# Linear attention and SwiGLU on one core: batch 0 loaded in order and contracted by head pairs, batches 2 and 3 prepared later

## The chip, the core and the metric

The kernel runs on one core of a Trainium2 chip. The core has five engines, each with its own in-order instruction queue: PE (matrix multiply, with weight loads shown apart as PEld), DVE (vector), ACT (scalar functions), POOL, and SP, which here only issues transfers. Transfers run on 16 DMA engines. Those issued by SP stand in one queue and those issued by POOL in another; here POOL's bring the weights from float32 to bf16 on the way, and some of SP's transpose. The metric is the device time of one execution in microseconds; of several runs the median counts.

## The reference, cut to what matters

Eight batches of 8 heads, 576 positions and 64 values per head. The attention has no softmax: its sums over positions are taken first.

```python
def phi(x, c, s):                       # c, s: cos and sin of a position's angle
    r = np.maximum(x, 0.0)
    return np.concatenate([r * c, r * s], axis=-1)
q_p, k_p = phi(q, cos_w, sin_w), phi(k, cos_w, sin_w)
kv  = np.einsum('bhsf,bhsd->bhfd', k_p, v)
z   = np.sum(k_p, axis=2)
num = np.einsum('bhsf,bhfd->bhsd', q_p, kv)
den = np.einsum('bhsf,bhf->bhs', q_p, z)[..., None] + 1e-06
x   = num / den                         # then to 4608 rows of 512
xn  = x / sqrt(mean(x * x) + 1e-06) * rms_g
out = (silu(xn @ w_gate) * (xn @ w_val)) @ w_out      # 512 -> 1536 -> 512
```

## The kernel before

**Tiles and names.** Of a batch's 576 positions 512 make four tiles of 128 rows (j or c = 0 to 3). The last 64 are the rest; the rests of two batches share one tile (j = 4), so odd batches have five tiles and even ones four. raw holds a batch's q, k or v as it was loaded (8 heads on 128 partitions, six buffers), remq, remk and remv the rests. qp and kp are relu(q) and relu(k) times cos and sin in bf16, 128 columns per head; vv is v in bf16 with a column of ones, which makes z beside kv. There is one kp, one vv and one qpT (qp transposed) for all batches; qpr and qprT are the same for the rests of q.

**Attention of a batch.** k_prep and v_prep fill kp and vv. kvz multiplies them for four heads at a time (20 matmuls) into one PSUM tile and copies the result to kvzs. nd(b, j) multiplies qpT with kvzs into a PSUM tile of the pool att, which has one buffer. x_of(b, j) makes x from it: on DVE den, rec and the product xt; on ACT the sum of squares (scr, ssq); on POOL the power that gives rs. xn_scale multiplies xt with rs and gb on DVE; xn_tr transposes the result by a transfer on SP, xn_tr_pe on PE with a copy on ACT, into xnT.

**FFN.** Eight blocks, one per batch, and a ninth for the rests. A block has 12 steps. gval(blk, nn) is one: 8 matmuls (gps and vps, 128 x 512), silu on ACT (sil), a product on DVE (hT). gps and vps have two PSUM buffers each. outp(blk, ...) multiplies hT with w_out, 48 matmuls a block, 4 beside each gval of the next block; store copies the result (osb) and sends it out. Block 0's output projection stands by itself behind its gval, four PSUM tiles at once, with what batch 1 still lacks among its 12 steps.

**Order.** Nothing is reordered: each engine runs what the program lists for it, in that order, and the program is written out by hand. At the start the loads of q, k, v and the weights of gate and value (wg, wv) are issued, almost all by POOL; batch 0 is prepared and contracted, and block 0 starts tile by tile (first_steps). Then attention_beside(b, r) is called behind each step of the blocks: r counts steps from the start of block b - 1, and is negative in the blocks before it. Batch 2 (batch2_beside) and batch 3 are both prepared beside block 1, batch 4 to 7 each beside the last five steps of block b - 2 and the first nine of block b - 1.

**Queues.** POOL's queue holds the loads and the rs of every x_of, in the program's order: a load behind an rs waits until that x_of is done. SP's holds the transposes of q, rests and xn, and the stores. A queue's ninth transfer waits until its first has landed.

## Time and profile before

| | us |
|---|---|
| runs | 364.98, 369.48, 369.74 |
| median | 369.48 |
| the profiled execution | 370.0 |
| its span | 368.2 |
| granted PE clock, mean of the span | 0.962 |
| PE busy in the span | 322.9 (88%), 2096 matmuls |
| DVE, ACT, POOL busy | 197.2, 156.5, 98.0 |
| read from and written to HBM | 38.01 MB, 9.44 MB |

The span is what the trace covers, in one profiled execution; its own time, 370.0 us, is 1.8 us longer and half a microsecond above the median. Times in the timeline count from the span's start. A row gives start, duration, engine, line, operation, output <- inputs, shapes and a count; in brackets stands how long the engine was idle before it and which instruction or transfer ended that. Durations of two neighbours on an engine may overlap a little, so distances between starts say more than durations. A matmul is called gps, vps, acc, kvz, nd, tps (transpose of qp) or tpx (transpose of xn) by the tile that it writes.

### The profile page before, as it was taken

The page shows a single profiled execution, that of the slowest core. Times are in us where ns is not written, and L with a number is a line of the kernel's source. Part 1 is how long each engine was busy: PE and PEld are TensorE (multiplying, and loading weights), DVE is VectorE, ACT ScalarE, POOL GpSimd, SP SyncE. Part 2 cuts the span into 40 slices and gives each one's busy share as a digit, 9 for nine tenths or more (in the row PEclk, how much of TensorE's full clock was granted, in tenths as well). Part 3 has the DMA queues.
Part 4 walks back from the last instruction along what each step waited for, and adds up shares of the span by engine and source line. Part 5 has one row for each costly group of instructions (what it writes and reads, how often), then busy time and mean ns, then how long its engine had stood idle before and what let it go on. Part 6 is the DMA issues. An engine that isn't in the chain of part 4 may idle for free.

```text
span 368.2 us, 5681 instructions
## 1 busy us (share of the span) xinstructions
PE 322.9 (88%) x2096; PEld 161.3 (44%) x2096; DVE 197.2 (54%) x420; ACT 156.5 (43%) x310; POOL 98.0 (27%) x145
## 2 busy tenths in 40 slices
PE   0459998985854999999999999799899999999995
PEld 0448454432421544444445445344444444444442
DVE  3654576463694369747954795486567222323210
ACT  2725484585434344534363445242535232332321
POOL 8317320342244036404901490161011000000000
PEclk9856999998996999999999999999999999999999
DMA  7999999569279438995995899999513200001013
GB/s 229 242 208 211 256 306 268 120 181 199 40 145 174 113 94 163 217 212 127 189 257 158 172 204 108 201 170 204 116 45 73 71 28 30 28 28 59 30 57 86
DMA packets 61611, 53.58 MB, mean 146 GB/s; under 512 B 44944, under 2 KB 50064, under 8 KB 61584
## 3 DMA queue, kind: packets, MB, share of 16 engines
q0 software_dynamic: 13024, 32.51, 38.0%
q1 hardware_dynamic: 48560, 20.72, 28.9%
q8 instruction: 16, 0.26, 0.3%
q14 instruction: 11, 0.09, 0.1%
HBM read 38.01 MB, written 9.44 MB: 129 GB/s over the span
## 4 chain that ended last, share of the span: by engine, by line
PE 56%; DMA 16%; DVE 12%; ACT 8%; issue 4%; POOL 2%; ACTq 0%; SPq 0%; DVEq 0%; POOLq 0%
PE gps L310 17%; PE vps L310 17%; PE acc L347 15%; DMA raw<-in_v_dram 9%; DMA qpT<-qp 5%; PE kvz L199 3%; DVE hT L319 3%; ACT sil L318 2%; PE nd L227 2%; ACT scr L253 2%; ACT vv L137 2%; DVE kp L130 2%; POOL raw L91 1%; PE acc L546 1%; DVE rec L242 1%
## 5 line engine op out<-in xcount | busy, mean ns | idle before, releaser
L319 DVE TENSOR_TENSOR hT<-vps,sil 128x512 bf16<-128x512 f32 x108 | 74.3, 689 | 131.1 <-PE vps L310 90.6
L310 PE MATMUL gps<-xnT,wg 128*128 128x512 bf16 (+1 forms) x408 | 102.3, 376 | 7.2 <-ACT xnT L137 5.0
L310 PE MATMUL vps<-xnT,wv 128*128 128x512 bf16 (+1 forms) x408 | 102.4, 376 | 0.0
L347 PE MATMUL acc<-wo,hT 128*128 128x512 bf16 x384 | 96.7, 380 | 0.0
L318 ACT ACTIVATE sil<-gps 128x512 bf16<-128x512 f32 x108 | 63.8, 591 | 64.8 <-PE gps L310 64.8
L310 PEld LDWEIGHTS <-wv 128*128 128x128 bf16 x456 | 44.8, 101 | 51.5 <-issue 2.5
L258 POOL TENSOR_TENSOR rs<-ssq,mhalf 128x1 f32<-128x1 f32 x36 | 20.4, 566 | 167.3 <-ACT scr L253 167.3
L310 PEld LDWEIGHTS <-wg 128*128 128x128 bf16 x456 | 41.9, 100 | 48.2 <-issue 9.6
L347 PEld LDWEIGHTS <-hT 128*128 128x128 bf16 x384 | 37.7, 98 | 45.6 <-issue 0.5
L329 ACT COPY osb<-acc 128x512 f32<-128x512 f32 x36 | 20.8, 584 | 27.8 <-PE acc L347 26.1
L199 PE MATMUL kvz<-vv,kp 128*128 128x65 bf16 x320 | 15.1, 200 | 11.9 <-DVE vv L139 4.7
L137 ACT CAST vv<-raw 128x512 bf16<-128x512 f32 x28 | 16.2, 623 | 20.3 <-DMA raw<-in_v_dram 20.3
L227 PE MATMUL nd<-kvzs,qpT 128*128 128x65 bf16 x256 | 14.3, 200 | 8.7 <-DMA qpT<-qp 2.5
L199 PEld LDWEIGHTS <-kp 128*128 128x128 bf16 x320 | 13.4, 102 | 16.9 <-issue 5.8
L227 PEld LDWEIGHTS <-qpT 128*128 128x128 bf16 x256 | 12.3, 102 | 17.1 <-DMA qpT<-qp 3.0
L130 DVE TENSOR_SCALAR qp<-raw,cos_tab 128x512 bf16<-128x512 f32 x32 | 16.6, 528 | 3.2 <-issue 3.2
L91 POOL DMA_DIRECT2D raw<-in_q_dram x23 | 17.7, 775 | 1.1 <-POOLq L589 0.8
L91 POOL DMA_DIRECT2D raw<-in_v_dram x23 | 17.5, 761 | 1.9 <-DMA wo<-in_moe_w_out_dram 1.4
L91 POOL DMA_DIRECT2D raw<-in_k_dram x23 | 17.6, 764 | 0.2 <-issue 0.2
L130 DVE TENSOR_SCALAR kp<-raw,cos_tab 128x512 bf16<-128x512 f32 x32 | 15.6, 502 | 0.4 <-DMA raw<-in_k_dram 0.3
L170 PE MATMUL tps<-ident,qp 128*128 128x128 bf16 x64 | 6.2, 262 | 9.5 <-ACT qp L128 9.3
L310 PE MATMUL vps<-xnT_104,wv 128*128 128x512 bf16 x48 | 12.3, 379 | 0.0
(78 smaller groups left out, 250.7 us busy)
## 6 DMA issues: line engine op xcount, KB each, us to landing
out_dram<-osb SPq DMA_DIRECT2D x32, 256.0 KB, 3.0
raw<-in_q_dram POOLq DMA_DIRECT2D x20, 256.0 KB, 8.8
raw<-in_k_dram POOLq DMA_DIRECT2D x20, 256.0 KB, 4.1
raw<-in_v_dram POOLq DMA_DIRECT2D x20, 256.0 KB, 4.5
raw<-in_k_dram POOLq DMA_DIRECT2D x3, 1024.0 KB, 10.6
raw<-in_v_dram POOLq DMA_DIRECT2D x3, 1024.0 KB, 16.2
raw<-in_q_dram POOLq DMA_DIRECT2D x2, 1024.0 KB, 12.8
wg<-in_moe_w_gate_dram POOLq DMA_DIRECT2D x3, 512.0 KB, 16.9
```

The costliest lines, as they stand in the source:

```text
L91: eng.dma_start(out=raws[what, b][:, h0 : h0 + n, :], in_=src[b, h0 : h0 + n, 0:SM, :].rearrange("h (p j) d -> p h (j d)", j=NJ),)
L130: nc.vector.tensor_scalar(out=dst, in0=src, scalar1=tab[lanes, col : col + 1], scalar2=0.0, op0=ALU.mult, op1=ALU.max,)
L137: nc.scalar.copy(out=dst, in_=src)
L199: nc.tensor.matmul(ps[:, half, hh * DE : (hh + 1) * DE], lhsT=kp[:, c, h, :], rhs=vv[:, c, h, :], start=(c == 0), stop=(c == NJ),)
L227: nc.tensor.matmul(ps[rows, h // HH, (h % HH) * DE : (h % HH + 1) * DE], lhsT=src[:, h, cols], rhs=kz[:, h, :], start=True, stop=True,)
L253: nc.scalar.activation(out=scr[:, :], in_=xt[:, :], func=AF.Square, scale=DM**-0.5, accum_out=ssq[:, :],)
L258: nc.gpsimd.tensor_tensor(out=rs[:, :], in0=ssq[:, :], in1=mhalf[:, :], op=ALU.pow)
L310: nc.tensor.matmul(ps[:, c0 : c0 + n], lhsT=w[:, dt, nn * P : (nn + 1) * P], rhs=xnTs[blk][:, dt, c0 : c0 + n], start=(dt == 0), stop=(dt ...
L318: nc.scalar.activation(out=sil[:, :], in_=gps[:, :], func=AF.Silu)
L319: nc.vector.tensor_tensor(out=hTs[blk][:, nn, :], in0=vps[:, :], in1=sil[:, :], op=ALU.mult)
L329: nc.scalar.copy(out=osb[:, :], in_=acc[:, :])
L347: nc.tensor.matmul(acc[:, :], lhsT=hTs[blk][:, nn, j * P : (j + 1) * P], rhs=wo[:, nn, :], start=(nn == 0), stop=(nn == NNT - 1),)
```

## The change

**The start.** Batch 0's q comes in four pieces of two heads, k in two halves and v in four pieces, all from SP, in this order, with gb behind. POOL issues the rests of k and v, then copies one element of v's second piece (gate), and behind that copy the weights; the rest of q follows much later. v is cast by head pairs (v_prep_heads), and kvz_heads contracts two heads at a time (10 matmuls), ACT and DVE taking turns.

**Behind it.** Batch 1's v is loaded ahead of w_out. qr_prep of batches 0 and 1, k_prep and v_prep of batch 1 change steps, and kvz(1) moves from behind step 2 of block 0's output projection to behind step 0; nd, x_of, xn and their transposes each move one step ahead there. kvz(2, 0) moves a step later, and nd(1, 4), x_of and xn of the first pair of rests go from block 1 to the first two steps of block 2.

**Batch 3** gets a plan of its own: loads in halves in steps 3 to 8 of block 1 (before: quarters, from two steps before block 1 to its step 9), q from step 10 of block 1 (before: 7), k from step 11 (before: 8), v in steps 0 and 1 of block 2 (before: 10 of block 1 on), kvz in steps 2 and 3 (before: 1 and 2), nd from step 4 (before: 3).

**The plan.** The steps of batches 4 to 7 are the same as before, now from a table. Within a step the table's order is xn, q, k, v, kvz, nd; before it was q, k, v, kvz, nd, xn.

```diff
+    def v_prep_heads(b, h0, n, eng):
+        src = raws["v", b][:, h0 : h0 + n, :].rearrange("p h (j d) -> p j h d", j=NJ)
+        copy(eng, vv[:, 0:NJ, h0 : h0 + n, 0:D], src)
...
-    def kvz(b, half, eng=nc.scalar):
+    def kvz_heads(b, h0, n, eng):
...
+        g, hh = divmod(h0, HH)
+        for h in range(h0, h0 + n):
             for c in range(NJ + 1):
                 nc.tensor.matmul(
...
+    def kvz(b, half, eng=nc.scalar):
+        kvz_heads(b, half * HH, HH, eng)
...
-    load_piece("q", q, 0, 0, 2, nc.sync)
-    load_piece("q", q, 0, 2, 2, nc.sync)
-    load_piece("q", q, 0, HH, HH, nc.gpsimd)
-    nc.gpsimd.iota(iota_i[:, :], pattern=[[0, 1]], base=0, channel_multiplier=1)
-    masks.make_identity(nc, ident[:, :])
-    load("k", k, 0)
-    load("v", v, 0)
+    for e in range(4):
+        load_piece("q", q, 0, 2 * e, 2, nc.sync)
+    for e in range(2):
+        load_piece("k", k, 0, HH * e, HH, nc.sync)
+    for e in range(4):
+        load_piece("v", v, 0, 2 * e, 2, nc.sync)
...
+    nc.gpsimd.iota(iota_i[:, :], pattern=[[0, 1]], base=0, channel_multiplier=1)
+    masks.make_identity(nc, ident[:, :])
+    load_rest("k", k, 0, nc.gpsimd)
+    load_rest("v", v, 0, nc.gpsimd)
+    nc.gpsimd.tensor_copy(out=gate[:, :], in_=raws["v", 0][:, 2, 0:1])
     for s in range(0, DFF, 512):
         load_wgv(s)
-    load_rest("q", q, 0, nc.gpsimd)
...
-    for c in range(NJ + 1):
-        v_prep(0, c, A if c % 2 else V)
-    kvz(0, 0, A)
-    kvz(0, 1, V)
+    v_prep(0, NJ, V)
+    for e in range(4):
+        v_prep_heads(0, 2 * e, 2, A if e % 2 else V)
+        kvz_heads(0, 2 * e, 2, V if e % 2 else A)
...
-    load("q", q, 1)
-    load("k", k, 1)
-    load_wout(0)
-    load_wout(1)
-    load("v", v, 1)
-    load_wout(2)
+    load_rest("q", q, 0, nc.gpsimd)
+    for what, src in (("q", q), ("k", k), ("v", v)):
+        load(what, src, 1)
+    for s in range(3):
+        load_wout(s)
...
+    PLAN = plan_of(
+        xn=each(4, 5), q=each(-5, 5), k=each(-4, 5), v=((-2, (0, 1)), (-1, (2, 3)), (0, (4,))),
+        kvz=each(1, 2), nd=each(3, 5),
+    )
+    PLAN_3 = plan_of(
+        xn=each(5, 5), q=each(-2, 5), k=((-1, (0,)), (0, (1, 2)), (1, (3, 4))),
...
-        if r in (1, 2):
-            kvz(b, r - 1)
-        if 3 <= r <= 6:
-            nd(b, r - 3)
-            x_of(b, r - 3)
...
-        if 4 <= r <= 7:
-            xn(b, r - 4)
...
+        plan = PLAN_3 if b == 3 else PLAN
+        for what, n in plan.get(r, ()):
...
+        if b == 3 and r == 0:
+            nd(1, NJ)
+            x_of(1, NJ)
+        if b == 3 and r == 1:
+            xn(1, NJ)
...
-        if nn == 2:
+        if nn == 0:
             kvz(1, 0, A)
             kvz(1, 1, V)
```

Each row of the following lists is an instruction of one engine: line, operation, output <- inputs with their buffer numbers, shape.

ACT at the contraction of batch 0, before: the last two copies of qpT, k's sines, its share of v, and the copy of the first four heads of kvz.

```order
L137 COPY qpT_101<-tps_196 128x8x128
L137 COPY qpT_101<-tps_216 128x8x128
L128 ACTIVATE kp_94<-raw_123,sin_tab_107 128x8x64 x4
L137 CAST vv_95<-raw_127 128x8x64 x2
L137 CAST kvzs_242<-kvz_241 128x260
L253 ACTIVATE scr_299,ssq_300<-xt0_96 128x513
```

And now:

```order
L138 COPY qpT_101<-tps_201 128x8x128
L138 COPY qpT_101<-tps_221 128x8x128
L129 ACTIVATE kp_94<-raw_120,sin_tab_107 128x8x64 x4
L138 CAST kvzs_244<-kvz_243 128x130
L138 CAST vv_95<-raw_123 128x4x2x64
L138 CAST kvzs_244<-kvz_243 128x130
L138 CAST vv_95<-raw_123 128x4x2x64
L260 ACTIVATE scr_306,ssq_307<-xt0_96 128x513
```

The copy of a pair's kvz stands ahead of the cast of the next pair's v that this engine does.

DVE in block 1, from batch 2's second xn to its third, before: hT is the FFN's product, qp and kp with raw_899 and raw_1014 are batch 3's.

```order
L319 TENSOR_TENSOR hT_918<-vps_1189,sil_1198 128x512
L266 SCALAR_TENSOR_TENSOR xn_1208<-xt0_96,rs_1181,gb_93 128x512
L237 TENSOR_SCALAR den_1219<-nd_1210 128x8
L242 RECIPROCAL rec_1221<-den_1219 128x8
L245 TENSOR_TENSOR xt1_97<-nd_1210,rec_1221 128x512
L130 TENSOR_SCALAR qp_1230<-raw_899,cos_tab_106 128x8x64
L130 TENSOR_SCALAR qp_1230<-raw_899,sin_tab_107 128x8x64
L130 TENSOR_SCALAR kp_94<-raw_1014,cos_tab_106 128x8x64
L130 TENSOR_SCALAR kp_94<-raw_1014,sin_tab_107 128x8x64
L319 TENSOR_TENSOR hT_918<-vps_1237,sil_1246 128x512
L266 SCALAR_TENSOR_TENSOR xn_1255<-xt1_97,rs_1227,gb_93 128x512
```

And now:

```order
L326 TENSOR_TENSOR hT_924<-vps_1159,sil_1168 128x512
L273 SCALAR_TENSOR_TENSOR xn_1178<-xt4_100,rs_1154,gb_93 128x512
L244 TENSOR_SCALAR den_1189<-nd_1180 128x8
L249 RECIPROCAL rec_1191<-den_1189 128x8
L252 TENSOR_TENSOR xt0_96<-nd_1180,rec_1191 128x512
L326 TENSOR_TENSOR hT_924<-vps_1203,sil_1212 128x512
L273 SCALAR_TENSOR_TENSOR xn_1221<-xt0_96,rs_1197,gb_93 128x512
```

Batch 3's q and k are gone from these steps; hT, xn and x_of keep their order.

DVE in block 3, batch 4's second x_of (den, rec, xt) between two hT, before:

```order
L319 TENSOR_TENSOR hT_1781<-vps_1929,sil_1938 128x512
L237 TENSOR_SCALAR den_1954<-nd_1945 128x8
L242 RECIPROCAL rec_1956<-den_1954 128x8
L245 TENSOR_TENSOR xt4_100<-nd_1945,rec_1956 128x512
L266 SCALAR_TENSOR_TENSOR xn_1964<-xt3_99,rs_1925,gb_93 128x512
L319 TENSOR_TENSOR hT_1781<-vps_1970,sil_1979 128x512
```

And now:

```order
L326 TENSOR_TENSOR hT_1784<-vps_1932,sil_1941 128x512
L273 SCALAR_TENSOR_TENSOR xn_1948<-xt3_99,rs_1928,gb_93 128x512
L244 TENSOR_SCALAR den_1961<-nd_1952 128x8
L249 RECIPROCAL rec_1963<-den_1961 128x8
L252 TENSOR_TENSOR xt4_100<-nd_1952,rec_1963 128x512
L326 TENSOR_TENSOR hT_1784<-vps_1973,sil_1982 128x512
```

xn of the first tile moved from behind the second tile's x_of to ahead of it.

More of the change, by code (lines that the diff above doesn't have):

```diff
@@ L81 @@
     iota_f = consts.tile([P, 1], FP32, name="iota_f")
+    gate = consts.tile([P, 1], FP32, name="gate")
     mhalf = consts.tile([P, 1], FP32, name="mhalf")
@@ L445, with plan_of, each @@
     gval_end(0, 1)
-    load("q", q, 1)
-    load("k", k, 1)
-    load_wout(0)
-    load_wout(1)
-    load("v", v, 1)
-    load_wout(2)
+    load_rest("q", q, 0, nc.gpsimd)
[3 more added lines that the diff above has]
+        load_wout(s)
     for what, src in (("q", q), ("k", k), ("v", v)):
         load(what, src, 2)
+    def plan_of(**firsts):
+        plan = {}
+        for what, steps in firsts.items():
+            for r, ns in steps:
+                for n in ns:
+                    plan.setdefault(r, []).append((what, n))
+        return plan
+    def each(r0, n):
+        return [(r0 + i, (i,)) for i in range(n)]
+    PLAN = plan_of(
[4 more added lines that the diff above has]
+        xn=each(5, 5), q=each(-2, 5), k=((-1, (0,)), (0, (1, 2)), (1, (3, 4))),
+        v=((0, (0, 1, 2)), (1, (3, 4))), kvz=each(2, 2), nd=each(4, 5),
+    )
     def attention_beside(b, r):
@@ L460, in attention_beside @@
         pieces = {}
-        if b > 2:
+        if b == 3:
+            for i, (what, src) in enumerate((("q", q), ("k", k), ("v", v))):
+                for e in range(2):
+                    pieces[-9 + 2 * i + e] = (what, src, HH * e, HH)
+        if b > 3:
             for i, (what, src) in enumerate((("q", q), ("k", k), ("v", v))):
@@ L525 @@
         gval(0, nn)
-        if nn == 2:
+        if nn == 5:
             qr_prep(0)
+        if nn == 9:
+            qr_prep(1)
         if 6 <= nn <= 9:
@@ L535 @@
             k_prep(1, 1, V, A)
-            qr_prep(1)
+            k_prep(1, 2, V, A)
         if nn == 11:
-            for c in range(2, NJ + 1):
-                k_prep(1, c, V, A)
+            k_prep(1, 3, V, A)
+            k_prep(1, NJ, V, A)
+            for c in range(NJ + 1):
+                v_prep(1, c, A if c % 2 else V)
     for j in range(NJ):
         accs[0, j] = pools["gv"].tile([P, DM], FP32, name="acc", tag="gv"[j % 2])
-    for c in range(NJ + 1):
-        v_prep(1, c, A if c % 2 else V)
     for nn in range(NNT):
```

61 lines of the change are left out of this document (26 added, 35 removed).

## The prediction

> **What bounds the kernel now.** I read the windows by stage first (start:end, length, busy time and instructions of PE, PEld, DVE, ACT, POOL, then PE clock, DMA share, GB/s), then, for each window with an idle PE, the timeline of the engine that PE waited for. The first window is the start up to batch 0's first nd, the second the output projection of block 0, and each from 71.49 on one FFN block.
>
> ```profile
> 0.00:22.09 22.09, 6.69 (x73) 5.88 (x73) 10.40 (x38) 10.46 (x17) 10.45 (x19) 0.87 0.98 231
> ...
> 54.27:71.49 17.22, 14.98 (x139) 7.76 (x137) 10.70 (x25) 8.94 (x21) 3.63 (x6) 1.00 0.81 185
> 71.49:115.27 43.78, 28.48 (x201) 13.24 (x201) 26.23 (x57) 23.11 (x48) 16.72 (x24) 0.92 0.73 154
> 115.27:150.92 35.65, 35.65 (x233) 17.14 (x233) 23.68 (x51) 13.42 (x29) 13.35 (x19) 0.95 0.65 134
> 150.92:185.33 34.41, 33.59 (x217) 16.34 (x216) 23.40 (x50) 15.80 (x33) 14.16 (x21) 1.00 0.85 191
> 185.33:219.29 33.96, 33.96 (x233) 16.73 (x232) 24.04 (x51) 14.74 (x33) 13.36 (x19) 1.00 0.89 196
> 219.29:255.28 35.99, 33.49 (x218) 16.24 (x216) 23.32 (x50) 14.64 (x31) 9.59 (x15) 1.00 1.07 164
> 255.28:291.01 35.73, 34.29 (x234) 16.77 (x232) 19.48 (x39) 15.96 (x34) 2.75 (x5) 1.00 0.37 88
> ```
>
> PE is idle 15.4 us of the start and 15.3 us of block 1; from block 2 on it is the bound, with 0 to 2.5 us idle per block. Block 4 has no idle at all and takes 33.96 us, 2.83 a step: that is PE's own pace. So the change can win in the first 115 us, where it takes work out of block 1, and it can lose in blocks 2 to 6, where it puts that work and where PE has nothing left to give. Below I carry one number along, the lead: how much earlier than before PE stands at the same instruction (minus is earlier).
>
> **The start.** From the timeline (start, us, engine, line; in brackets the idle time before it and what ended it) and the DMA issues of the first 20 us (last number: us to landing):
>
> ```profile
> 1.28 0.92 POOL L91 DMA_DIRECT2D raw<-in_q_dram  x1 [0.83 <-POOLq L589]
> 8.54 2.56 ACT L128 ACTIVATE qp<-raw,sin_tab 128x512 bf16<-128x512 f32 x4 [4.49 <-DMA raw<-in_q_dram]
> 13.18 1.80 DVE L130 TENSOR_SCALAR kp<-raw,cos_tab 128x512 bf16<-128x512 f32 x4 [0.31 <-DMA raw<-in_k_dram]
> 14.13 2.56 ACT L128 ACTIVATE kp<-raw,sin_tab 128x512 bf16<-128x512 f32 x4
> 17.43 1.14 ACT L137 CAST vv<-raw 128x512 bf16<-128x512 f32 x2 [0.73 <-DMA raw<-in_v_dram]
> 19.82 0.38 ACT L137 CAST kvzs<-kvz 128x260 bf16<-128x260 f32 x1 [1.25 <-PE kvz L199]
> 20.24 1.26 PE L199 MATMUL kvz<-vv,kp 128*128 128x65 bf16 x20 [0.46 <-ACT kvzs L137]
> 28.89 0.59 PE L310 MATMUL gps<-xnT,wg 128*128 128x128 bf16 x4
> ```
> ```profile
> raw<-in_k_dram POOLq DMA_DIRECT2D x1, 1024.0 KB, 10.3
> raw<-in_q_dram SPq DMA_DIRECT2D x2, 256.0 KB, 2.8
> ```
> ```profile
> 2.00:4.00 2.00, 0.00 (x0) 0.00 (x0) 1.28 (x9) 0.59 (x4) 1.83 (x6) 1.00 1.01 297
> ```
>
> Today each stage waits for its load: q at 8.54, k at 13.18, v at 17.43. SP's two pieces of q land 2.8 us after issue, at 297 GB/s. Four 0.26 MB pieces at that rate take 0.88 us apart, so q is complete at 0.74 + 2.8 + 2.65 = 6.2; k's 1.05 MB and the two rests' 0.26 MB add 4.4 (10.6); v ends at 14.1. ACT then starts q 2.3 us earlier (8.54 - 6.2); its four qp, two copies and four kp follow one another as now, so it ends kp at 14.13 + 2.56 - 2.3 = 14.4, and DVE, free of q at 10.5, has its kp by then. From there v is no longer late; the chain of head pairs is the bound. Each pair is 10 matmuls (0.63 by the x20 row), a copy (about 0.3, from 0.38 for 260 columns) and the next pair's cast (0.42 to 0.6), which stands behind that copy on the same engine: PE, copy, cast, PE, one after the other. The waits that make it so are there today: the second half of kvz starts 0.04 us after ACT's copy of the first (19.82 + 0.38 to 20.24), though it writes another bank. Four times 0.63, four copies of 0.3, three casts of 0.5 and eight hand-overs of 0.07 make 5.8 us; nd starts at 20.2, not 22.09, where the first window ends: **-1.9** (ends: 0 if k comes 2 us later, -2.6 if the queue runs faster than 297).
>
> The weights wait behind the gate on POOL, with the rs operations behind them. The gate opens at about 11.6 (2.9 MB at 297 GB/s), the six issues end by 17, the first pair of weights (1 MB) lands by about 19, and is read at 28.89 - 1.9: nothing lost, and 8 us of cover if the gate opens late. Batch 0's rest of q goes onto POOL's queue behind batch 0's rs, ahead of batch 1's loads: one more issue in front of these, hidden, since batch 1's q is first read in step 6 of the block, four steps of gval on; its own reader, qr_prep(0), moved three steps later. w_out's issues move behind v1's two (0.75 us each, by the x3 row further down), and are first read at 54.27, ten steps on: hidden as well. The iota ahead of POOL's loads gives the tables 0.9 us earlier, which q hides. Two queues carry what one carried; gb, last on SP behind v, is read only by xn, which needs nd, x_of and rs first.
>
> The Trainium skill, DMA: Bandwidth & Descriptors, section Issuing engines are not separate DMA queues, says that issuing from other engines saves only issue time, since all run on the same 16 DMA engines. By that rule the start would win only the 0.92 us issue ahead of the iota, and the sum below would be 373.0. The 2.8 against 10.3 us rows speak for more.
>
> **The output projection of block 0.**
>
> ```profile
> 54.27 3.03 PE L546 MATMUL acc<-wo,hT 128*128 128x512 bf16 x12
> 57.51 0.42 DVE L139 CAST vv<-remv 64x512 bf16<-64x512 f32 x1
> 57.31 1.31 PE L199 MATMUL kvz<-vv,kp 128*128 128x65 bf16 x20
> ```
>
> kvz(1) moves from behind the third step to behind the first. But vv is done at 57.9 (57.51 + 0.42), whatever PE does: DVE and ACT carry the same q, k and v preparation as before from step 8 of the block on, qr_prep and k_prep only change places among the steps. So PE does 4 of these 12 matmuls (1 us), and then waits 2 us for vv where it waited almost nothing. The 8 matmuls it could have done there come behind kvz (8 x 0.25 = 2.0 by the x12 row, of which the wait before was nothing); the chain nd, x_of, xn starts behind two of these steps, and two bare steps stand behind it instead of one: **+2.0** (ends 0, if vv is ready sooner, and +2.5). The lead is then -1.9 + 2.0 = +0.1.
>
> **Block 1.**
>
> ```profile
> 74.54 0.60 ACT L318 ACTIVATE sil<-gps 128x512 bf16<-128x512 f32 x1
> 77.79 0.63 ACT L253 ACTIVATE scr<-xt_99 128x513 bf16<-128x513 f32 x1 [1.43 <-DVE xt_99 L245]
> 78.42 0.58 ACT L318 ACTIVATE sil<-gps 128x512 bf16<-128x512 f32 x1
> 87.44 0.64 PE L199 MATMUL kvz<-vv,kp 128*128 128x65 bf16 x16 [1.50 <-ACT vv L137]
> 91.94 1.03 PE L310 MATMUL gps<-xnT,wg 128*128 128x512 bf16 x4
> 115.27 1.87 PE L310 MATMUL gps<-xnT,wg 128*128 128x512 bf16 x4 [4.96 <-ACT xnT L137]
> ```
>
> ACT is the bound from 74.54 to 87.44. nd(1,4)'s square and the wait for it leave (1.43 + 0.63 + 0.1 = 2.2), so kvz(2) comes at 87.44 + 0.1 - 2.2 = 85.4. Step 5's gval now stands before it, hidden in that wait, and the next gval starts at 87.2, not 91.94: lead -4.7. Then the x_of steps:
>
> ```profile
> 98.69 0.69 DVE L245 TENSOR_TENSOR xt_96<-nd,rec 128x512 f32<-128x512 f32 x1
> 99.50 0.64 ACT L253 ACTIVATE scr<-xt_96 128x513 bf16<-128x513 f32 x1 [2.54 <-DVE xt_96 L245]
> 100.13 0.58 ACT L318 ACTIVATE sil<-gps 128x512 bf16<-128x512 f32 x1
> 100.74 0.69 DVE L319 TENSOR_TENSOR hT<-vps,sil 128x512 bf16<-128x512 f32 x1 [0.57 <-ACT sil L318]
> 101.35 0.74 DVE L266 SCALAR_TENSOR_TENSOR xn<-xt_96,rs,gb 128x512 bf16<-128x512 f32 x1
> 102.44 0.69 DVE L245 TENSOR_TENSOR xt_97<-nd,rec 128x512 f32<-128x512 f32 x1
> ```
>
> This is a closed loop: x_of, its square, the next sil behind it on ACT, hT, xn, the next x_of: 3.75 us a step. The idle in front of hT (0.57, ended by sil) shows that DVE waits inside the loop; batch 3's q and k lay in that wait, so taking them out shortens it little (0.2 in all over three steps). The gain is behind the loop: ACT no longer sits on v3 before the copy of batch 2's last xnT, and of the 4.96 us that PE waited for that copy only some 0.4 is left (the copy itself). Block 2 starts at 105.8: lead -4.7 - 0.2 - 4.6 = **-9.5** (ends -7, if the new loads of batch 3 are late, and -12, if the loop gets shorter too). Batch 3's loads in halves stand on POOL behind fewer rs than the quarters did and are read 3 steps later or more: hidden.
>
> **Block 2** pays back. DVE gets 12 of the q and k operations (0.45 each by the x4 row) and nd(1,4) in its first two steps, so kvz(3) waits about 2.7 us for k; nd(1,4) costs PE 0.4; the first eight matmuls are no longer at half clock (-1.7). nd(3,0) stands one step later (+2.8): its x_of comes 9.5 - 2.7 - 0.4 + 1.7 - 2.8 = 5.3 us earlier than before. And the plan now runs xn ahead of x_of in every step of batches 3 to 7. In the old order the loop is shorter:
>
> ```profile
> 167.54 0.69 DVE L245 TENSOR_TENSOR xt_100<-nd,rec 128x512 f32<-128x512 f32 x1
> 170.62 0.69 DVE L245 TENSOR_TENSOR xt_96<-nd,rec 128x512 f32<-128x512 f32 x1
> ```
>
> 3.08, against 3.75 with xn inside. So in every batch each x_of falls 0.66 us further behind than the one before it, and the rs on POOL with it. On POOL the loads of the next batch's v stand in order behind these rs. From the timeline, the last of these loads, the casts that wait for them, and the one nd that waited for a transpose:
>
> ```profile
> 143.88 2.25 POOL L91 DMA_DIRECT2D raw<-in_v_dram  x3
> 151.94 1.14 ACT L137 CAST vv<-raw 128x512 bf16<-128x512 f32 x2 [4.48 <-DMA raw<-in_v_dram]
> 184.40 1.14 ACT L137 CAST vv<-raw 128x512 bf16<-128x512 f32 x2 [2.58 <-DMA raw<-in_v_dram]
> 236.37 0.43 PE L227 MATMUL nd<-kvzs,qpT 128*128 128x65 bf16 x8 [2.50 <-DMA qpT<-qp]
> ```
>
> rs(3,4) comes 5.3 - 4 x 0.66 = 2.7 us earlier, one piece less (0.75) stands behind it: v4's cast, which already waits 4.48 us, starts 3.5 us earlier, 4.0 if it lands a little faster. Lead at block 3's third step **-4.0** (ends -2 and -8).
>
> **Blocks 3 to 6.** PE has 2.83 us a step, the loop 3.75: with one att buffer nd(3) waits about 0.5 and nd(4) 0.9 more. v5 lands 3 x 0.66 = 2.0 later; its wait is 2.58, of which PE feels nothing before, so about 0.5 is slack: **+1.5** in block 3, **+2.7** in block 4 (five nd: 4 x 0.66), in block 5 1.3 less half of a wait for qpT that may absorb it (2.50): **+0.4** (ends -0.6 and +2), in block 6 0.5 + 0.9 = **+1.4**, with no loads behind it.
>
> Sum: -4.0 + 1.5 + 2.7 + 0.4 + 1.4 = +2.0. The profiled execution took 370.0 us (368.2 span, 1.8 around it), 0.5 above the median of 369.48: **372.0**, no measurable change.
>
> **Rivals.** *The loop is not closed* (faster): sil gets ahead of the square and PE sets the pace. For it: before, blocks 3 and 4 ran at PE's pace at 3.08; against: 3.75 in batch 2. Blocks 3 to 6 lose nothing (-6.0), batch 2's three steps save 0.9 each (-2.7), v4 comes 2 earlier: 361.3. *The clock falls* (slower): the new waits of 2 to 2.8 us before kvz(1), kvz(2), block 2, kvz(3) and block 3's second step grow past the length that halves the clock. The wait of 2.50 at 236.37 did not halve it (window 1.00), that of 4.96 did: the four matmuls after it take 1.87 instead of 1.03. Eight such matmuls cost 1.7, five places 8.5: 380.5. It decides if the waits exceed some 3 to 4 us. The Trainium skill, TensorE: Matmul & The Clock Gate, section Part 1: The HAM clock gate, puts the limit at an idle window of about 3.4 us; by that rule the waits above stay warm, and both rows agree. *The head pairs gain nothing* (the change does not do what it says): k lands 2 us later than I reckon: 373.9.
>
> **How the numbers follow.** Forecast 0.55, loop not closed 0.20, head pairs 0.12, clock 0.13. A measurement of this kernel tells about 2% from no change (362.1 to 376.9): faster 0.20, same 0.67, slower 0.13. The range 361 to 378 takes in all but the clock and the ends of the block terms.
>
> **What would show it.** nd of batch 0 near 20.2; kvz(1) waiting 2 us for vv; block 2 starting near 106; x_of in batches 3 to 7 every 3.75 us, not 3.08; vv waits for v of 3 to 5 us. x_of at 2.9 to 3.1 us, or no wait at nd(3) and nd(4), would make it wrong.

## The result, and the profile after

The changed kernel is slower. Its median is 380.7 us (380.1 to 382.2, four runs) against 369.5 for the kernel before in the same session: a ratio of 1.034, 95% interval 1.026 to 1.043. The forecast was 372.0, with a range of 361 to 378, so the time lies outside it. The profiled execution took 381.1 us, with a span of 379.3 (370.0 and 368.2 before). One run of a version below took 436.8 us at a granted clock of 0.77, where the other three took 360.0 to 364.6: its median is given without that run (the expectations have 362.8, with it), and all ratios are of undisturbed runs alone.

First the windows by stage of the changed kernel, cut at the same instructions as those of before (columns as there):

```profile
0.00:22.53 22.53, 6.80 (x73) 5.82 (x74) 9.76 (x39) 10.30 (x18) 7.49 (x16) 0.87 0.95 226
54.61:73.48 18.87, 15.02 (x137) 7.76 (x137) 10.30 (x24) 9.03 (x21) 5.16 (x8) 1.00 0.73 195
73.48:111.64 38.16, 27.20 (x181) 12.74 (x184) 19.57 (x41) 21.20 (x43) 7.34 (x11) 0.96 0.53 142
111.64:152.46 40.82, 36.57 (x243) 17.47 (x248) 29.84 (x67) 14.97 (x33) 15.38 (x22) 0.96 0.76 145
152.46:191.08 38.62, 33.78 (x212) 16.23 (x217) 23.55 (x50) 14.91 (x32) 15.71 (x23) 1.00 0.78 167
191.08:226.63 35.55, 34.11 (x228) 16.74 (x233) 22.88 (x48) 15.05 (x33) 12.15 (x18) 1.00 0.80 184
226.63:266.24 39.61, 35.29 (x214) 16.76 (x217) 24.62 (x53) 15.97 (x34) 10.89 (x16) 0.96 1.13 165
266.24:301.63 35.39, 33.95 (x229) 16.67 (x232) 19.50 (x39) 14.81 (x33) 2.75 (x5) 1.00 0.32 81
```

Block 1 takes 38.2 us instead of 43.8, as its lighter load lets one expect. Block 2 takes 40.8 instead of 35.7, and blocks 3 to 6, each at PE's pace or 2 us above it before, take 149.2 instead of 140.1 (sums of their four lengths). PE's busy time there grew by 1.8 us, the time in which it is idle by 7.3. The timeline of the changed kernel shows where PE stands and what it waits for, with one row of ACT:

```profile
22.53 0.59 PE L234 MATMUL nd<-kvzs,qpT 128*128 128x65 bf16 x8 [0.45 <-DVE kvzs L140]
57.85 1.31 PE L203 MATMUL kvz<-vv,kp 128*128 128x65 bf16 x20 [1.34 <-DVE vv L140]
80.57 1.09 PE L317 MATMUL vps<-xnT,wv 128*128 128x512 bf16 x4 [4.34 <-ACT osb L336]
93.09 0.81 PE L317 MATMUL gps<-xnT,wg 128*128 128x512 bf16 x3
152.46 1.04 PE L317 MATMUL gps<-xnT,wg 128*128 128x512 bf16 x4 [1.23 <-DMA xnT<-xn]
155.33 1.14 ACT L138 CAST vv<-raw 128x512 bf16<-128x512 f32 x2 [7.14 <-DMA raw<-in_v_dram]
157.01 1.02 PE L317 MATMUL gps<-xnT,wg 128*128 128x512 bf16 x4 [1.78 <-ACT sil L325]
161.41 0.81 PE L317 MATMUL gps<-xnT,wg 128*128 128x512 bf16 x3
176.18 0.42 PE L234 MATMUL nd<-kvzs,qpT 128*128 128x65 bf16 x8 [0.49 <-DVE xt_96 L252]
191.08 1.02 PE L317 MATMUL gps<-xnT,wg 128*128 128x512 bf16 x4 [1.53 <-DMA xnT<-xn]
215.75 0.58 PE L234 MATMUL nd<-kvzs,qprT 128*64 128x65 bf16 x16 [0.73 <-DVE xt_96 L252]
```

There are three kinds of wait. Those at nd (0.49, 0.73) are the ones the forecast named, and so is the one for a silu (1.78), which stands on ACT behind casts waiting for v (7.14): it is the wait before block 3's second step. The wait of 4.34 us at 80.57 stands in no part of the forecast, and nor do those for xnT at a block's first step (1.23, 1.53).

DVE's timeline has the step of the loop in the same stretch:

```profile
167.88 0.69 DVE L252 TENSOR_TENSOR xt_99<-nd,rec 128x512 f32<-128x512 f32 x1
171.60 0.69 DVE L252 TENSOR_TENSOR xt_100<-nd,rec 128x512 f32<-128x512 f32 x1
```

Two x_of are 3.72 us apart, where they were 3.08 apart before.

### The profile page after: what moved, and what is told of

It is laid out like the page before. It is cut to its first block, busy times and chain, and to the rows that moved or that the text cites. A ratio compares the mean times of both kernels' runs of the same rounds, so it can differ in the third digit from the quotient of the medians.

```text
span 379.3 us, 5654 instructions
## 1 busy us (share of the span) xinstructions
PE 323.8 (85%) x2060; PEld 161.3 (43%) x2096; DVE 196.5 (52%) x421; ACT 155.7 (41%) x311; POOL 91.5 (24%) x137
## 4 chain that ended last, share of the span: by engine, by line
PE 53%; DMA 14%; DVE 14%; ACT 10%; issue 6%; POOL 1%; SPq 0%; another core or an unknown queue 0%; ACTq 0%; DVEq 0%
PE gps L317 16%; PE vps L317 16%; PE acc L354 14%; DMA qpT<-qp 6%; ACT sil L325 3%; DVE xn L273 3%; PE kvz L203 3%; ACT scr L260 2%; DMA xnT<-xn 2%; PE nd L234 2%; ACT kp L129 2%; DMA raw<-in_v_dram 2%; DMA out_dram<-osb 2%; DVE kp L131 2%; PE acc L578 2%
## 5 line engine op out<-in xcount | busy, mean ns | idle before, releaser
L317 PE MATMUL gps<-xnT,wg 128*128 128x512 bf16 (+1 forms) x390 | 99.8, 376 | 7.3 <-ACT sil L325 3.0
L92 POOL DMA_DIRECT2D raw<-in_k_dram x20 | 15.2, 762 | 2.3 <-DMA raw<-in_v_dram 1.9
L92 POOL DMA_DIRECT2D raw<-in_q_dram x20 | 15.5, 776 | 0.4 <-issue 0.4
L92 POOL DMA_DIRECT2D raw<-in_v_dram x20 | 15.2, 761 | 0.1
L260 ACT ACTIVATE scr<-xt_96 128x513 bf16<-128x513 f32 x8 | 5.1, 635 | 19.1 <-DVE xt_96 L252 19.1
```

Source lines behind the costliest of these rows:

```text
L92: eng.dma_start(out=raws[what, b][:, h0 : h0 + n, :], in_=src[b, h0 : h0 + n, 0:SM, :].rearrange("h (p j) d -> p h (j d)", j=NJ),)
L260: nc.scalar.activation(out=scr[:, :], in_=xt[:, :], func=AF.Square, scale=DM**-0.5, accum_out=ssq[:, :],)
L317: nc.tensor.matmul(ps[:, c0 : c0 + n], lhsT=w[:, dt, nn * P : (nn + 1) * P], rhs=xnTs[blk][:, dt, c0 : c0 + n], start=(dt == 0), stop=(dt ...
```

## The experiments

Each run is compared with runs of the kernel before on the same chip. "Ratio" is to that kernel, with its 95% interval.

### The place of xn in the step

In the first run xn stands last in the tables again, in the second the one edit is made to the kernel before.

```diff
-        xn=each(4, 5), q=each(-5, 5), k=each(-4, 5), v=...
-        kvz=each(1, 2), nd=each(3, 5),
+        q=each(-5, 5), k=each(-4, 5), v=...
+        kvz=each(1, 2), nd=each(3, 5), xn=each(4, 5),
```

> The changed kernel with the scaling and transpose of a subtile put back behind the next subtile's nd and x_of in each step (batches 3 to 7). Theory 1 (order within the step closes a loop of 3.75 us over x_of, square, sil, hT, xn): x_of follow each other by 3.1 us, the nd waits of 0.5 and 0.7 us go, the later loads come earlier, and blocks 2 to 6 lose about 1 instead of 7 us on before: 373 to 376 us. Rival (blocks 2 to 6 lose by loads and transposes that land late for other reasons): the waits on DMA stay and the time is 379 to 382 us.

Measured: 368.9 us, ratio 1.001 (0.997 to 1.006). DVE's timeline of this run has the shorter step:

```profile
167.91 0.69 DVE L252 TENSOR_TENSOR xt<-nd,rec 128x512 f32<-128x512 f32 x1
170.97 0.69 DVE L252 TENSOR_TENSOR xt<-nd,rec 128x512 f32<-128x512 f32 x1
```

The whole loss is gone: this one edit is worth 12 us, about twice what was expected here, and the rest of the change comes to nothing in sum.

> The kernel before with that one edit alone: xn ahead of nd and x_of in each step of batches 3 to 7. Theory 1: x_of every 3.75 us, 5 to 7 us slower than before, 374 to 377 us. Rival (before has slack in its DMA that the changed kernel lost): no more than 2 us slower.

Measured: 382.2 us, ratio 1.037 (1.031 to 1.044). The edit alone, without anything else of the change, makes the kernel before as slow as the changed one, 13 us where 5 to 7 were expected.

The next run asked why. It leaves xn ahead but a step later.

```diff
-        xn=each(4, 5), q=each(-5, 5), ...
+        xn=each(5, 5), q=each(-5, 5), ...
```

> The changed kernel with xn still ahead of nd and x_of in its step, but one step later (steps 5 to 9 instead of 4 to 8, in batch 3 steps 6 to 10), so that the rs it waits for is a step old. Theory 1 (the loss is the loop: xn waits for an rs whose square stands behind this step's sil, and x_of stands behind that xn): the loop is open, x_of follow each other by about 3.1 us, the nd waits go, and the time is 368 to 373 us. Rival (0.7 us of DVE work ahead of x_of is what delays it, whenever its rs was ready): no more than 3 us faster than the changed kernel, 377 to 380 us.

Measured: 395.6 us, ratio 1.074 (1.067 to 1.080): 15 us slower than the changed kernel, where both theories wanted it faster. The timeline of this run shows a step on DVE, and the rs that its xn reads:

```profile
174.55 0.56 POOL L265 TENSOR_TENSOR rs<-ssq,mhalf 128x1 f32<-128x1 f32 x1 [19.12 <-ACT scr L260]
...
172.95 0.69 DVE L252 TENSOR_TENSOR xt<-nd,rec 128x512 f32<-128x512 f32 x1
176.01 0.69 DVE L252 TENSOR_TENSOR xt<-nd,rec 128x512 f32<-128x512 f32 x1
178.06 0.69 DVE L326 TENSOR_TENSOR hT<-vps,sil 128x512 bf16<-128x512 f32 x1 [1.35 <-ACT sil L325]
178.66 0.74 DVE L273 SCALAR_TENSOR_TENSOR xn<-xt,rs,gb 128x512 bf16<-128x512 f32 x1
179.76 0.69 DVE L252 TENSOR_TENSOR xt<-nd,rec 128x512 f32<-128x512 f32 x1
```

The batch's first two x_of, with no xn between them yet, are 3.06 us apart (172.95 to 176.01). The next two are 3.75 apart (176.01 to 179.76), although the xn between them has an rs that had been ready for 3.5 us (174.55 + 0.56 to 178.66). So the wording of this expectation was wrong and that of the prediction right: rs is not in the loop. The loop is xt, square, the silu behind it, hT, xn, xt, and xn lengthens it by 0.7 us, about its own duration, though what it reads is ready. The further 15 us come mostly from elsewhere, from the transposes of xn and PE behind them (timelines of the same run):

```profile
191.14 1.60 SPq L288 DMA_TRANSPOSE xnT<-xn  x1
...
203.15 1.87 PE L317 MATMUL gps<-xnT,wg 128*128 128x512 bf16 x4 [9.18 <-DMA xnT<-xn]
```

The last xn of the batch ends on DVE at 188.98. Its transpose goes out 2.2 us later, behind the next batch's first qpT and a store, and PE starts the block that reads it 12.0 us after that. In between POOL issues eight loads of 256 KB and two rests (185.65 to 193.35); what part of the 12 us is theirs was not tested. PE waits 9.18 us, after which its first matmuls run at half speed (1.87 instead of 1.02), and 4.08 us at 279.78 for block 6's. xnT for a block lands only just in time; that is the point at which a late xn is paid for.

The price of xn's place without the other losses is seen in a pair: the version with three edits (below) and the same with xn ahead.

> The changed kernel with batch 3's loads held and kvz of batch 1 behind step 2, but with xn ahead of nd and x_of as in the change: against the kernel with all three edits (362.8 us) this is the price of xn's place alone, where block 1 loses nothing. Theory 1: x_of every 3.75 us and nd waits of 0.5 and 0.7 us in batches 3 to 7, each block's first steps wait for xnT or the sil behind it, 8 to 12 us slower than with xn behind: 371 to 375 us. Rival (part of that price was batch 3's loads and the stores): 366 to 369 us.

Measured: 374.5 us, ratio 1.017 (1.008 to 1.026), against a ratio of 0.981 (0.975 to 0.987) with xn behind. The windows of blocks 3 to 6, first with xn behind (only the line that sums and averages the four):

```profile
sum 136.79, PE 135.17 PEld 66.14 DVE 89.82 ACT 61.63 POOL 39.96; mean PE 33.79 PEld 16.54 DVE 22.45 ACT 15.41 POOL 9.99
```

and with xn ahead:

```profile
147.74:185.40 37.66, 33.77 (x212) 16.24 (x217) 23.81 (x51) 14.74 (x32) 15.77 (x23) 1.00 0.83 168
185.40:221.12 35.72, 34.12 (x228) 16.70 (x233) 22.89 (x49) 15.22 (x33) 12.35 (x19) 1.00 0.79 186
221.12:258.25 37.13, 33.77 (x213) 16.23 (x216) 24.42 (x53) 14.77 (x32) 10.88 (x16) 1.00 0.99 166
258.25:293.94 35.69, 34.13 (x229) 16.70 (x234) 19.41 (x39) 15.79 (x34) 2.75 (x5) 1.00 0.36 90
```

Length less PE's busy time is 1.6 us in sum with xn behind and 10.4 with xn ahead. Blocks 3 and 5 lose most of it at a block's first steps: PE's timeline has waits of 1.27 and 1.23 us there for the silu behind v's casts, and of 1.09 and 0.61 for the next block's xnT. Blocks 4 and 6 lose 1.6 us each, 0.50 + 0.74 of it in the two nd waits of block 4. PE's clock is 1.00 in all of them.

### Batch 3's loads and block 0's stores

The wait of 4.34 us at 80.57 is followed back in the timeline of POOL, ACT and SP in the changed kernel:

```profile
70.01 0.79 POOL L92 DMA_DIRECT2D raw<-in_q_dram  x1
70.97 0.77 POOL L92 DMA_DIRECT2D raw<-in_q_dram  x1 [0.17 <-issue]
...
72.42 0.76 POOL L92 DMA_DIRECT2D raw<-in_k_dram  x1
72.84 1.56 ACT L336 COPY osb<-acc 128x512 f32<-128x512 f32 x3 [0.49 <-PE acc L578]
73.45 7.42 SPq L339 DMA_DIRECT2D out_dram<-osb  x4
79.94 0.58 ACT L336 COPY osb<-acc 128x512 f32<-128x512 f32 x1 [5.53 <-DMA out_dram<-osb]
```

Block 0's four output tiles are copied to osb, which has three buffers; the fourth copy waits until the first store has landed, and PE waits for that copy, since gps and vps share PSUM buffers with these tiles. Three loads of half a batch went out just ahead of the stores. DMA issues between 60 and 95 us, changed kernel (last number: us to landing):

```profile
out_dram<-osb SPq DMA_DIRECT2D x4, 256.0 KB, 6.6
```

Before, the same row reads:

```profile
out_dram<-osb SPq DMA_DIRECT2D x4, 256.0 KB, 2.7
```

And POOL's timeline before:

```profile
68.67 1.46 POOL L91 DMA_DIRECT2D raw<-in_q_dram  x2
78.60 0.56 POOL L258 TENSOR_TENSOR rs<-ssq,mhalf 128x1 f32<-128x1 f32 x1 [8.47 <-ACT scr L253]
79.12 1.53 POOL L91 DMA_DIRECT2D raw<-in_q_dram  x2
```

Two quarters of q went out at 68.67 and the next loads only at 79.12, behind the rs of nd(1,4), which stood in block 1's step 0. The change moved that rs away and with it what had held the loads. Two runs test this: one holds the loads by a copy on POOL that reads block 1's hT, the other puts nd(1,4) back.

```diff
+        if b == 3 and r == -9:
+            nc.gpsimd.tensor_copy(out=gate[:, :], in_=hTs[1][:, 1, 0:1])
```

> The changed kernel with one copy of 128x1 on GpSimd ahead of batch 3's loads, which reads hT of block 1's step 1, so that the loads leave only after block 0's four stores have been issued. Theory 2 (the loads that GpSimd issues at 70.0 to 73.2 us share the DMA engines with the stores; the fourth output copy waits for a store's landing): the wait of 4.34 us at 80.57 us goes, block 1's seventh step starts near 89 instead of 93 us, and if it is carried to the end the time is 376 to 377 us. Rival (the gain is given back where batch 3's q and k are then late): the wait goes, the time is 379 to 382 us.

Measured: 376.3 us, ratio 1.020 (1.013 to 1.027). The stores land in 2.7 us again, and PE's wait for that copy, at 76.56 in this run, is 0.49 us. Block 1's seventh step starts at 89.73, and 4.4 us are won between the medians (374.0 to 378.1 in this version's four runs, 380.1 to 382.2 in those of the changed kernel): theory 2 holds, and the gain is carried to the end.

```diff
-        if b == 3 and r == 0:
-            nd(1, NJ)
-            x_of(1, NJ)
-        if b == 3 and r == 1:
-            xn(1, NJ)
+        if r == 0:
+            nd(1, NJ)
+            x_of(1, NJ)
+        if r == 1:
+            xn(1, NJ)
```

> The changed kernel with the odd row group of batches 0 and 1 (nd, x_of, xn with index 4 of batch 1) back in block 1's steps 0 and 1, where it was before. Theory 2 (it was this x_of's power on GpSimd that held batch 3's loads behind block 0's stores): stores land in about 3 us instead of 6.6, the wait of 4.34 us at 80.57 us goes, the square costs the ScalarE chain 2 us again: 377 to 380 us. Rival (the stores are slow whatever GpSimd issues): the wait stays and the time is 381 to 384 us.

Measured: 376.7 us, ratio 1.022 (1.015 to 1.029), the stores at 2.7 us, and PE's wait of 4.34 us is gone. Batch 3's first load goes out at 84.19, right behind the rs of nd(1,4) (83.69, 0.55 us). It was that rs which had held the loads, though nothing in the program says so.

### The output projection of block 0

```diff
-        if nn == 0:
+        if nn == 2:
             kvz(1, 0, A)
             kvz(1, 1, V)
```

> The changed kernel with batch 1's kvz, nd, xn and their transposes in the output projection of block 0 where they stood before (kvz behind step 2 and not step 0, the others a step later). Theory: PE's wait of 1.34 us for vv goes and with it the lower clock behind it; block 1 starts 1.2 to 1.8 us earlier against block 0's end than in the changed kernel (19.4 instead of 21.06 us behind gps of step 11). Rival: the wait is work that has to end anyway and returns at nd: no more than 0.5 us.

Measured: 381.3 us (one run). From gps of step 11 (52.77) to block 1's first (72.37) are 19.60 us instead of 21.06: the 1.5 us are there, and the wait for vv is gone. But the stores now land in 7.7 us, PE's wait for osb is 5.46 us, and nothing is left at the end (in this one run). A gain ahead of a wait that ends by a transfer is no gain until that wait is dealt with.

The three edits together (xn behind, loads held, kvz(1) back):

> The changed kernel with three edits together: xn behind x_of again, batch 3's loads held behind block 0's stores, batch 1's kvz behind step 2 again. If the three losses are separate and what is left of the change gains: 362 to 366 us, 1 to 2% under before. Rival (what was lost at one place is regained at the next, since block 2 waits for batch 3's loads): 367 to 370 us.

Measured: 360.9 us, ratio 0.981 (0.975 to 0.987). The losses are separate: 12, 4.4 and 1.5 us make 18 in sum, and the version is 20 us under the changed kernel. Its ratio, 2% under the kernel before, has 1 outside the interval.

### The start

Four runs looked at the term that was forecast as -1.9 and came out as +0.4. In the changed kernel ACT starts q at 8.50, not 6.2, and each group of kvz but the first waits 0.8 to 0.9 us for a cast (here the second):

```profile
8.50 2.56 ACT L129 ACTIVATE qp<-raw,sin_tab 128x512 bf16<-128x512 f32 x4 [6.07 <-DMA raw<-in_q_dram]
18.27 0.71 PE L203 MATMUL kvz<-vv,kp 128*128 128x65 bf16 x10 [0.88 <-ACT vv L138]
```

The first of these runs lets SP issue the rests of k and v behind v.

```diff
+    load_rest("k", k, 0, nc.sync)
+    load_rest("v", v, 0, nc.sync)
...
-    load_rest("k", k, 0, nc.gpsimd)
-    load_rest("v", v, 0, nc.gpsimd)
```

> The changed kernel with the rests of k and v of batch 0 issued by SP behind v's pieces instead of by GpSimd at 1.5 and 2.3 us. Theory 3 (the rests' 256 B packets, which GpSimd's queue moves beside q's pieces, are what makes q's last piece land at 8.5 us): q is complete at 6 to 6.7 us and the first nd starts at 20.2 to 21 instead of 22.5 us. Rival (k's pieces, issued 2 us behind q's, share the engines with them): q is complete at 8 to 8.6 us, nd within 0.5 us of 22.5.

Measured: 381.9 us (one run). ACT starts q at 6.77, as theory 3 has it, but nd at 22.84: DVE waits for the rest of k.

```profile
15.20 0.49 DVE L131 TENSOR_SCALAR kp<-remk,cos_tab 64x512 bf16<-64x512 f32 x1 [2.42 <-DMA remk<-in_k_dram]
```

The second issues the casts ahead of the pairs, on top of the three edits.

```diff
     for e in range(4):
         v_prep_heads(0, 2 * e, 2, A if e % 2 else V)
+    for e in range(4):
         kvz_heads(0, 2 * e, 2, V if e % 2 else A)
```

> The kernel with the three edits together, and batch 0's four casts of v by head pairs issued ahead of the four pairs' matmuls and copies, where each cast but the first stood behind the copy of the pair two or one before it. Theory (the head pairs are a chain PE, copy, cast, PE of 1.5 us a link, and this order is what makes it one): the four groups of kvz matmuls follow each other by 0.7 instead of 1.5 us, the first nd starts near 20 instead of 22.1 us, and the time is 360 to 361.5 us. Rival (the pairs wait for v's or k's data): the groups stay 1.5 us apart or start later, and the time is that of the three edits, 362 to 364 us.

Measured: 360.8 us, ratio 0.977 (0.970 to 0.984), the same time as with the three edits alone (360.9), so that the time speaks for neither and the trace has to tell. The groups are 1.29, 1.16 and 1.07 us apart, not 0.7:

```profile
16.85 0.71 PE L203 MATMUL kvz<-vv,kp 128*128 128x65 bf16 x10 [3.45 <-DVE vv L140]
18.14 0.71 PE L203 MATMUL kvz<-vv,kp 128*128 128x65 bf16 x10 [0.59 <-ACT kvzs L138]
19.30 0.71 PE L203 MATMUL kvz<-vv,kp 128*128 128x65 bf16 x10 [0.45 <-DVE kvzs L140]
20.37 0.71 PE L203 MATMUL kvz<-vv,kp 128*128 128x65 bf16 x10 [0.35 <-ACT kvzs L138]
```

The casts no longer wait, but each group waits for the copy of the one before. From the first group to nd are 4.7 us (16.85 to 21.53) instead of 6.1 in the changed kernel (16.43 to 22.53).

The third holds the rests behind q besides.

```diff
+    nc.gpsimd.tensor_copy(out=gate[:, :], in_=raws["q", 0][:, H - 1, 0:1])
     load_rest("k", k, 0, nc.gpsimd)
     load_rest("v", v, 0, nc.gpsimd)
```

> The kernel with the three edits and the casts ahead, and the rests of k and v of batch 0 issued by GpSimd behind a copy of 128x1 that reads q's last piece, so that they don't share the DMA engines with q. Theory 3 (the rests' packets are what made q's last piece land at 8.1 to 8.5 us): q is complete at 6.2 to 6.8 us; the rests land by 13 us, just when VectorE wants them, and the first nd starts about 1.5 us earlier than with the casts ahead alone: 358.5 to 360.5 us. Rival (the rests are then what is late, as when SP issued them): q is complete as early, VectorE waits for the rest of k, and nd comes no earlier.

Measured: 359.8 us, ratio 0.976 (0.968 to 0.983), nd at 20.96; but ACT starts q at 8.05, with no rest under way. Theory 3 doesn't hold here, though it did with the rests on SP. The fourth puts nothing but q on the engines at first.

```diff
-        load_piece("k", k, 0, HH * e, HH, nc.sync)
...
-        load_piece("v", v, 0, 2 * e, 2, nc.sync)
...
+    nc.gpsimd.tensor_copy(out=gate[:, :], in_=raws["q", 0][:, H - 1, 0:1])
+    load("k", k, 0)
+    load("v", v, 0)
```

> The kernel with the three edits and the casts ahead, and at the start nothing but q's four pieces on the DMA engines: k and v of batch 0, whole and with their rests, and the gains follow on GpSimd's queue behind a copy of 128x1 that reads q's last piece. Theory 4 (k's pieces, issued at 2.8 us, share the engines with q and make q's last piece land at 8 to 9 us): q is complete at 5.5 to 6.5 us, where 1 MB at some 370 GB/s from 2.5 us would end; k's main part lands by 10.5 us, when it is wanted, and the first nd starts at 19 to 21 us: 358 to 360.5 us. Rival (q's own four pieces are slow): q is complete at 7.5 us or later, k and v land later by as much, and nd starts at 22 to 24 us: 361 to 364 us.

Measured: 364.2 us, ratio 0.988 (0.981 to 0.996). q starts at 6.65, which is no better than 6.77 with k's pieces behind; k and v are then late and nd starts at 24.60, later than either side had it. So q takes until about 6.7 at best, and theory 4 has nothing to win. Over the runs with the new order and k's and v's pieces behind q, q came at 6.8, 6.8, 7.5 and 8.1 in four without early rests and between 8.1 and 9.2 in nine with them: the rests cost about 1 us, so theory 3 holds in part, and what makes up the remaining spread is not settled. Three of the four issue the same transfers in the same order and still differ by 1.3 us. Nor does an earlier q alone bring nd forward there: nd starts at 21.06 with q at 6.78 and at 20.96 with q at 8.05, since DVE waits for the rest of k.

Is the new start worth anything, then? The three edits with the old start:

```diff
-    for e in range(4):
-        load_piece("q", q, 0, 2 * e, 2, nc.sync)
...
+    load_piece("q", q, 0, 0, 2, nc.sync)
+    load_piece("q", q, 0, 2, 2, nc.sync)
+    load_piece("q", q, 0, HH, HH, nc.gpsimd)
...
+    kvz(0, 0, A)
+    kvz(0, 1, V)
```

> The kernel with the three edits (362.8 us) with the start of before: q's second half, k, v and the weights on GpSimd's queue without the hold, batch 0's v cast by its five parts and kvz in two halves. Theory (the new start gains nothing: first nd at 22.5 against 22.1 us): first nd at 21.8 to 22.6 us, the time within 2 us of the kernel with the new start, 360 to 364 us. Rival (the new start gains what was predicted, 2 us, and the trace of the changed kernel was an unlucky one): 364 to 366 us.

Measured: 359.2 us, ratio 0.977 (0.969 to 0.984), nd at 22.58. That is 0.8 us under the range of the theory, but it can't be told from the three edits (0.981), nor from the version with casts ahead and rests held (0.976), whose nd comes 1.6 us earlier. The new start gains nothing that these runs could show.

### Batch 3 prepared later

This part is undone by letting batch 3 use the table of the others, on top of the fastest version.

```diff
-        plan = PLAN_3 if b == 3 else PLAN
+        plan = PLAN
```

> The fastest version so far (three edits, casts ahead, rests held; 359.8 us) with batch 3 prepared by the same table as the later batches, three to four steps earlier and beside block 1's end, as before the change; its loads stay as they are. Theory 5 (preparing batch 3 later moves a cost from block 1 to block 2 and saves little): PE waits 3 to 6 us for batch 3's v at the end of block 1 again, block 2 takes 35 to 36 us instead of 38.9, and the time is 358 to 362 us. Rival (block 2 is long for other reasons, so that the later table is a gain): block 2 stays at 38 us or more and the time is 363 to 367 us.

Measured: 360.6 us, ratio 0.981 (0.975 to 0.987). In this run the odd row group of batches 0 and 1 is computed with the queries of batches 2 and 3, whose rests are transposed into qprT before nd(1,4) reads it. The next run has nd(1,4) in block 1, where it comes first.

> Batch 3 prepared early as in the run before, and the odd row group of batches 0 and 1 back in block 1's steps 0 and 1, so that it has read its queries before batch 3's overwrite them; batch 3's loads are held as before. Theory 5 (preparing batch 3 later saves nothing): PE waits 2 to 4 us for batch 2's last xnT at the end of block 1, block 2 takes 35 to 37 us, and the time is within 2 us of the 359.8 us of the version with batch 3 late. Rival (the odd group's square in block 1's ScalarE chain, 2 us, is carried to the end): 362 to 364 us.

Measured: 361.3 us, ratio 0.978 (0.970 to 0.987). Blocks 1 and 2, batch 3 early:

```profile
69.45:108.22 38.77, 26.64 (x198) 12.71 (x200) 26.01 (x57) 23.00 (x48) 14.42 (x21) 1.00 0.87 184
108.22:143.86 35.64, 35.26 (x228) 17.11 (x232) 23.68 (x51) 13.43 (x29) 13.35 (x19) 0.95 0.67 134
```

and late:

```profile
70.43:104.70 34.27, 25.84 (x181) 12.32 (x184) 19.74 (x41) 21.21 (x43) 10.85 (x16) 1.00 0.78 170
104.70:143.55 38.85, 34.85 (x244) 17.16 (x248) 30.74 (x68) 14.98 (x33) 16.76 (x24) 1.00 0.75 162
```

Late, block 1 is 4.5 us shorter and block 2 is 3.2 us longer; block 3 starts at 143.55 against 143.86, where the early version had stood 1 us ahead at block 1's start. Of the 4.5 us 1.3 are left, part of which may be nd(1,4) in block 1, and the times don't tell them from nothing. PE's wait for batch 2's last xnT, in front of 108.22, is 2.75 us. Theory 5 holds.

## Why the prediction was wrong

The loop that the prediction put at its centre is there. What failed is the sum around it: block 1's term above all, then the start, and less so block 2; in blocks 3 to 6 errors cancelled. The lead at the places that the forecast named or that follow from its terms, from PE's rows and windows above, against those of before (157.80 for block 3's third step):

| place | forecast | measured |
|---|---|---|
| nd of batch 0 | -1.9 | +0.4 |
| block 1, first gps | +0.1 | +2.0 |
| block 1, seventh gps | -4.7 | +1.2 |
| block 2, first gps | -9.5 | -3.6 |
| block 3, third gps | -4.0 | +3.6 |
| block 4, first gps | -2.5 | +5.8 |
| block 5, first gps | +0.2 | +7.3 |
| block 6, first gps | +0.6 | +11.0 |
| block 7, first gps | +2.0 | +10.6 |

Of the 8.6 us between the two ends, 2.3 arise at the start, -0.4 in the output projection, 4.0 in block 1, 1.7 in block 2 and 1.0 from there on.

- **The start failed**, by 2.3 us, at "q is complete at 0.74 + 2.8 + 2.65 = 6.2". It was complete at 8.5. Behind it no engine waits for a load until nd in the changed kernel's trace, so the 2.3 us are q's; no run had q early and the rests in time at once, so this is read and not tested. Alone on the engines q took 6.65, and early rests cost about 1 us; the rest of the delay stays open. The chain of head pairs was sized right (5.8 forecast, 6.1 measured), but it is longer than what it replaced: before, first kvz (17.91) to nd (22.09) took 4.2. The rival in which the head pairs gain nothing came true in its result, though it named k's load and not q's. The Trainium skill, DMA: Bandwidth & Descriptors, section Issuing engines are not separate DMA queues, says that transfers issued from several engines share the same DMA engines, so that another issuer saves only issue time. The forecast set a row of 2.8 against 10.3 us over that rule; the trace agrees with the rule, q starting at 8.50 with all of it issued by SP and at 8.54 with half of it issued by POOL.
- **The output projection of block 0 was nearly right**: +2.0 forecast, +1.6 measured, 1.34 of it the wait for vv; the run with kvz(1) moved back returned 1.5.
- **Block 1 failed in one sentence, and this is the largest miss**: "Batch 3's loads in halves stand on POOL behind fewer rs than the quarters did and are read 3 steps later or more: hidden." It asks when the loads are read, and puts at nothing what they share the DMA engines with. Fewer rs ahead of them is why they went out early, onto block 0's stores; it cost 4 us between block 1's first and seventh step, and with the loads held these steps won 4.0 of the 4.8 forecast. The rest of the block was right: from the seventh step to block 2 the lead grew by 4.8 as forecast, and the wait of 4.96 fell to 0.67.
- **Block 2 was undersized**: 5.5 forecast, 7.2 measured. kvz(3) waited less than forecast (1.4 in sum, not 2.7), but the wait of 1.23 for xnT at block 3's first step was missing, and the 1.7 that were taken off for the first eight matmuls did not come: PE's clock was 0.60 from 111.64 to 114.00 in the changed kernel, behind waits of 1.62 and 0.67. v4's first casts were forecast 3.5 to 4.0 us earlier than before and came 3.4 later (155.33 against 151.94); 5.9 of these 7 us were missing already at block 2's first step. The forecast followed the late rs to the loads behind it, but not to the transposes of xn that the next block reads.
- **Blocks 3 to 6 came out near by luck**: 1.5 + 2.7 + 0.4 + 1.4 = 6.0 forecast, 7.0 measured, but term by term 2.1, 1.6, 3.6 and -0.3. The nd waits were right (0.49 and 0.73 against 0.5 and 0.9). Block 5 was far off. Its working, 1.3 less half of 2.50, gives 0.05 and not the 0.4 in the sum; the wait for qpT was 2.03 and absorbed only 0.5; PE waited 1.26 for a silu and ran eight matmuls at half speed (1.8 us).
- **The closed loop of 3.75 us was right**, but the price of xn's place was not. The rival in which the loop is not closed comes out 372.0 - 361.3 = 10.7 us lower, of which 2.7 are batch 2's steps, whose order the change leaves alone; so the prediction priced xn's place at 8 us, and the runs gave 12 and 13. It set these 8 us off against a gain of 6 from the rest of the change, and by the first run the rest comes to nothing.
- **The clock is not the reason.** Its rival named 380.5, close to the time, but over blocks 1 to 6 the mean granted clock is 0.98 in both kernels. Its limit of some 3 to 4 us does not hold either: in the changed kernel a wait of 2.03 us in front of 248.50 was followed by half speed (four gps in 1.90 us), and the 2.50 us before the change, in front of 236.37, was not. What decides is open.

## What to carry to other kernels

On an in-order engine, an operation on the loop from one step's product to the next can cost its whole duration in every step, even if its own input was ready long ago: here 0.7 us of xn made 3.06 us 3.75. Put what can wait (a scaling, a copy) behind the operation that closes the loop. Before moving an operation, list the transfers that stood behind it on its queue: it may be what holds them off something else, as the rs of nd(1,4) held batch 3's loads off block 0's stores. A gain ahead of a wait for a transfer can be lost in that wait, so follow it to the first wait that a transfer ends before counting it.

## What the runs showed that was not expected

Stores of 256 KB took 6.6 us to land instead of 2.7 when three loads of 512 KB and a rest had been issued in the 3.5 us ahead of them, and 7.7 in the run with kvz(1) moved back. It is the same transfer in the same place, so a store's landing can't be taken for fixed.

1 MB of q, issued by SP in four pieces and alone on the DMA engines, was complete only at 6.65 us, and between 6.8 and 9.2 with other loads beside it, though in the run with q alone DMA moved 230 to 370 GB/s in most slices of that time.

PE's groups of kvz, which write different columns of one PSUM tile, waited 0.35 to 0.59 us for the copy of the group before. Whether the chip asks for that or only the program's ordering by tile was not tested.
